# A gated mix of a two-dimensional FFT filter and a GeGLU layer on one Trainium2 core: when a split product is copied, and where one group of an inverse stage is done

## The chip, the core and the metric

One core of a Trainium2 chip. The metric is device time in microseconds (us): the median of three runs of the whole kernel. The profile is of one further execution; its span goes from the first to the last instruction. The engines are TensorE (PE in the profile, its weight loads PEld), VectorE (DVE), ScalarE (ACT), GpSimd (POOL) and SyncE (SP, which here only issues DMAs). Each has its own queue and runs its instructions in order.

## What is computed

From the reference, cut to what matters; x is 2048 tokens of 576 features, `w_gate` and `w_up` are 576 x 4608, `w_down` is 4608 x 576:

```python
def reference(A_x, A_w_r, A_w_i, B_x, B_w_gate, B_w_up, B_w_down, gate_w):
    x = A_x
    g = _sigmoid((x * gate_w).sum(-1, keepdims=True))
    a = _A_ref(x, A_w_r, A_w_i)       # irfft2(rfft2(x) * (w_r + 1j * w_i))
    b = _B_ref(x, B_w_gate, B_w_up, B_w_down)   # (gelu(x wg) * (x wu)) wd
    return g * a + (1 - g) * b
```

All of it is float32. Each float32 factor of a matmul is split into a high part (float32r) and a low part, so one product takes three matmuls: high by high, low by high, high by low.

## The kernel before, in words

**Two strands.** The GeGLU layer fills TensorE; the filter (the spectral work) is done almost wholly by DVE and ACT beside it, as a Python generator from which pieces are taken while the program is written. The order on every engine's queue is therefore fixed by hand at build time (`manual_schedule`).

**The GeGLU strand.** The tokens are two halves of 1024 (p = 0, 1), the 4608 hidden features 18 groups (`PAIRS`) of 256. That makes 36 groups, q = 0 to 35; `PLAN` says how each is done: "c" is a direct group (`conv`, L1411), "s" a group by a Strassen scheme with seven products (`products`, L1197). The plan is 2 c, 10 s, 7 c, 17 s; so there are two Strassen stretches, starting at q = 2 and q = 19 (`starts`), and two direct stretches ahead of them.

A direct group does four hidden blocks (`hidden`, L923): for each of two token blocks tb of 512 and two blocks e of 128 features a gate chain and an up chain (`chain`, L878, 14 matmuls of 512 columns). GELU of the gate chain is done by ACT into `gl`; then `mult` on DVE multiplies it by the up chain's bank and frees that bank, `copy` on ACT makes the high part `hb[:, 0]`, and `low` on DVE (L944) the low part `hb[:, 1]`. A Strassen group does fourteen `seven`s (L1181, seven matmuls each; seven products, two halves s each); at n = 0 ACT copies each half's bank into the bank in which n = 1 goes on adding. A finished pair of hidden blocks goes on the list `pend`; `pop` takes from it and `down` (L973) does the down product: 12 matmuls of 288 columns, an ACT eviction into `stg` (L984) and an accumulating DMA into `yd` (POOL).

**Gaps.** `gap` (L774) is called after the first and third quarter of every chain, after every `seven` and after every `down`. It counts up, then issues (1) what `at(n, ...)` has put down for this count, in order of count and then of entry, (2) one entry of `aux`, (3) pieces of the spectral generator, as long as `credit` is positive. TensorE's work adds to the credit, each piece has a cost (0.69 us, 0.61 us and so on), and the credit is cut to 1.2 (2.0 during the columns) at each gap. A piece that yields None ends the gap. So a "gap later" means behind everything that was put on that engine's queue in between. `seq(key, (n, step), ...)` puts down steps for later gaps, and `due(key)` issues at once those that are still open. A down product calls `due` for both of its hidden blocks; `products` also does so for the last direct pair before its first seven (L1233).

**The spectral strand** (`spectral`, L675): rows forward for each half of the tokens, then `columns` (L255 on; forward column transform, weights, inverse column transform, beside the direct groups q = 12 to 18), then the inverse rows in the last stretch. The tile `til` holds 16 column tiles, four groups d of four. `beside` inside `columns` does the first inverse stage (`four` with sign +1: `_butterfly`, ten DVE instructions) for the groups d = 0 to 2 and stores each with `keep(d)`, four DMAs from til to `bw` in DRAM (L621). For d = 3 the end of `columns` does it: it loads the sources of the second half's Strassen operands into the tile `rows` (`load_part`, 8 DMAs), puts down the loads of the third part for two gaps later (4 DMAs, into tmp and orow), does `four(3, ...)`, `keep(3)`, and notes the count in `kept`:

```python
            for i in range(2):
                load_part(1, i)
            at(2, lambda: load_part(1, 2))
            yield from four(3, range(4), r[:, 0:SW], 1)
            keep(3)
            kept[0] = count[0]
```

Then `operands(1)` (L1051) makes the sums and their high parts (ACT, `sx`, which overwrites the place of `til`) and low parts (DVE). Its `steps` does the sums of part 0, waits until `count` is `kept[0] + HOLD` (HOLD = 5), puts the three high parts of part 2 on a list `acts`, and goes on with the sums of part 1; each piece that it yields first issues one entry of `acts`. After `until(3)`, that is in the last Strassen stretch, `fetch(e)` loads the four tiles of row block e from `bw` (L625), `late_tiles(e)` does the second inverse stage, and `inverse_rows` the rest and the output through `last_rows` (L570, and an accumulating DMA at L571). Before the last group (q = 35) whatever is left of the generator is issued with no GeGLU work between. In the last direct groups `reload_x` (L1404) brings x of the second half through `aux`: `prep_x` (L820) copies the high part on ACT (xhi<-wq and others), and puts down the low part on DVE (L826) for the next gap.

Of the kernel before, what the change touches and what calls it, by code (L numbers as in the profile page):

```python
# [26 lines left out]
SW = 2 * (KF + 1)  # L27
# [136 lines left out]
def _build(nc, tc, a):  # L164
    with ExitStack() as ctx:
# [3 lines left out]
        vec, act, pl, pe = nc.vector, nc.scalar, nc.gpsimd, nc.tensor  # L169
# [10 lines left out]
        _, loc = _block_of_token()  # L180
# [37 lines left out]
        def copy(o, i):  # L218
            act.activation(o, i, AF.Copy)  # L219
# [11 lines left out]
        def rows_tile():  # L231
            return pool.tile([P, ROWS], F32, name="rows", tag="rows")
# [6 lines left out]
        def columns():  # L239
# [141 lines left out]
            n = count[0]  # L381
# [7 lines left out]
            for i in range(2):  # L389
                load_part(1, i)  # L390
            at(2, lambda: load_part(1, 2))
            yield from four(3, range(4), r[:, 0:SW], 1)
            keep(3)
            kept[0] = count[0]

        re, im = slice(0, NK), slice(NK, SW)

# [3 lines left out]
        def four(d, at, sp, sgn):  # L401
            T = tiles()
            yield from _butterfly(vec, lambda i: T[:, d, i], lambda i: T[:, d, i, re], lambda i: T[:, d, i, im],
                                  at, sp, sgn, (0.69, 0.39))
# [204 lines left out]
        def until(n):  # L609
            while phase[0] < n:  # L610
                yield None
# [11 lines left out]
        def fetch(e):  # L623
            for d in range(4):
                nc.sync.dma_start(fetched[d], bw[:, SW * (4 * e + d):SW * (4 * e + d + 1)])  # L625

        def late_tiles(e):

            if e % 2 == 0:
                box[0] = rows_tile()  # L630
            rows = box[0]
            R = row_view(rows)
            x = [tmp[:, SW * i:SW * (i + 1)] for i in range(4)]
            src = list(fetched)
            *tmps, sp = (rows[:, i:i + SW] for i in (UNIT, UNIT + SW, 3 * UNIT, 3 * UNIT + SW))
            o = LEFT.index(e)
            if o:
                for k in range(1, 4):
                    c = 1.0 if o * k == 4 else math.sin(math.pi * o * k / 8)
                    act.activation(tmps[k - 1], src[k], AF.Copy, scale=c)  # L640
                    yield None
                for k in range(1, 4):
                    c, t, y = math.cos(math.pi * o * k / 8), tmps[k - 1], src[k]
                    if o * k == 4:
                        act.activation(x[k][:, re], t[:, im], AF.Copy, scale=-1.0)
                        copy(x[k][:, im], t[:, re])
                    else:
                        vec.scalar_tensor_tensor(x[k][:, re], y[:, re], c, t[:, im], op0=ALU.mult, op1=ALU.subtract)
                        yield 0.39
                        vec.scalar_tensor_tensor(x[k][:, im], y[:, im], c, t[:, re], op0=ALU.mult, op1=ALU.add)  # L650
                        yield 0.39
                    src[k] = x[k]
            n = 0
            for v in _butterfly(vec, lambda i: x[i], lambda i: x[i][:, re], lambda i: x[i][:, im],
                                range(4), sp, 1, (0.69, 0.39), src):
                yield v
                n += 1
                if n == 4 and e < 3:
                    yield None
                    fetch(e + 1)  # L660
            yield None
            s2 = sgn[:, None, :].to_broadcast([P, 2, KF])
            for n in range(2):
                g = 2 * (e % 2) + n
                pl.memset(rows.rearrange("p (c g k) -> p c g k", c=2, g=4)[:, :, g, 2 * KF:], 0.0)
                y = tmp[:, 2 * SW * n:2 * SW * (n + 1)].rearrange("p (t c k) -> p c t k", t=2, c=2)[:, :, :, 0:KF]
                copy(R[:, g, 0, :, 0:KF], y[:, 0])
                vec.tensor_tensor(R[:, g, 1, :, 0:KF], y[:, 1], s2, ALU.mult)
                yield 0.69
            yield None  # L670
# [4 lines left out]
        def spectral(rows):  # L675
# [63 lines left out]
            cols[0] = False  # L739
            yield from operands(1)  # L740
            yield from until(3)
            fetch(0)
            for _ in range(4):
                yield None
# [104 lines left out]
        def seq(key, *steps):  # L849

            q = todo[key] = [fn for _, fn in steps]
            for n, _ in steps:
                at(n, lambda: q and q.pop(0)())

        def due(key):
            q = todo.pop(key, [])
            while q:
                q.pop(0)()
# [64 lines left out]
        def hidden(q, e, tb, mid):  # L923

            i = hn[0]
            hn[0] += 1
            g = gl[i % 2]
            if i == 0:
                pg, pu = first_chains()
                act.activation(g, pg, AF.Gelu_apprx_tanh)  # L930
            else:
                pg = chain(q, e, 0, tb)
                act.activation(g, pg, AF.Gelu_apprx_tanh)
                mid()
                pu = chain(q, e, 1, tb)
            u = take()
            h = hb[u]

            def mult():
                vec.tensor_tensor(g, g, pu, ALU.mult)  # L940
                copy(h[:, 0], g)

            def low():
                vec.tensor_tensor(h[:, 1], g, f(h[:, 0]), ALU.subtract)  # L944

            credit[0] -= 1.22
            seq(("h", i), (1, mult), (3, low))
            return (q, e), u, ("h", i)

        def down_mm(ps, prev, t, part):  # L950
# [188 lines left out]
        def prep_b(q, m, lead=0):  # L1139

            if q >= len(PLAN) or PLAN[q] != "s":
                return
            w = slots[q, m]
            r11, r21, ts, r12, r22 = spots(q)
            x = (r11, r21, ts, r11, r12, r22, r21)[m]

            def high():
                copy(w[:, 256:1024], x)

            def low():  # L1150
                o = w.rearrange("p (c k) -> p c k", c=5)[:, 0:5:2]
                vec.tensor_tensor(o, x.rearrange("p (c k) -> p c k", c=3),  # L1152
                                  f(w[:, 256:1024]).rearrange("p (c k) -> p c k", c=3), ALU.subtract)

            def tail():
                copy(w[0:64, 512:768], x[0:64, 256:512])

            credit[0] -= 0.88
            seq(("b", q, m), (lead + 1, high), (lead + 3, low), (lead + 4, tail))
# [37 lines left out]
        def products(q):  # L1197
# [30 lines left out]
            def add(o, x, v):  # L1228
                vec.tensor_tensor(o, x, v, ALU.add)
                credit[0] -= 0.61  # L1230

            downs = (0, 0, 1, 0, 1, 1, 1) if q in starts else (1, 1, 1, 1, 1, 1, 2)
            if q in starts:  # L1233
                for _, _, key in pend[-1][0][3]:
                    due(key)
            for n, (name, nd) in enumerate(zip(("a11", "a12", "s2", "s1", "s3", "s4", "a22"), downs)):
                if q in starts and n == 0:
                    prep_b(q, 2, -1)
                m = n + 3
                if n in (1, 2):  # L1240
                    total(q, 4 - n)
# [277 lines left out]
```

## Time and profile before

| | us |
|---|---|
| runs | 1337.53, 1338.86, 1337.45 (median 1337.53) |
| the profiled execution, whole | 1338.92 |
| its span, first to last instruction | 1337.1 |
| TensorE (PE) busy | 1325.9 |
| DVE busy | 1141.0 |
| ACT busy | 862.5 |
| POOL busy | 267.3 |

Mean granted TensorE clock 0.998. Busy means that an instruction of the engine is under way; matmuls overlap, so a matmul of 512 columns is shown with some 390 ns though the next starts 227 ns later. Lines L219, L98, L103 and L106 belong to the helpers `copy` and `_butterfly`; there the tile names say which work it is. A row of the timeline gives start, duration, engine, line, operation, tiles out<-in, shape, count, and in brackets how long the engine was idle before and what ended that.

### The profile page before, as it was taken

How to read it: one execution, taken by the hardware profiler on the slowest of the kernel's cores; microseconds unless marked ns; L12 is line 12 of the kernel's file. 1: busy time of each engine (PE TensorE's matmuls, PEld its weight loads, DVE VectorE, ACT ScalarE, POOL GpSimd, SP SyncE). 2: the span in 40 equal slices, each digit the busy share in tenths (PEclk: the TensorE clock that was granted, in tenths of full speed). 3: DMA queues.
4: the chain of work that ended last, by engine and by line, in shares of the span. 5: the costliest groups of instructions: out<-in, count | busy, mean ns of one | idle time of the engine just before them, and what ended most of it. 6: DMA issues, size and time to landing. Idle time of an engine off the chain costs nothing.

```text
span 1337.1 us, 19999 instructions
## 1 busy us (share of the span) xinstructions
PE 1325.9 (99%) x7311; PEld 1172.6 (88%) x7311; DVE 1141.0 (85%) x1621; ACT 862.5 (65%) x1504; POOL 267.3 (20%) x341
## 2 busy tenths in 40 slices
PE   9999999999999999999999999999999999999998
PEld 7888888888888888989888888888888888888888
DVE  6899999899899688899778889999958999996554
ACT  5666766666665546777675776676577667667762
POOL 0011212212122222222211022121132212113211
PEclk9999999999999999999999999999999999999999
DMA  8667777876667978999985576766798676677977
GB/s 310 225 141 153 146 144 131 217 153 127 110 119 163 227 171 192 222 262 240 254 237 164 153 199 129 136 129 129 133 179 194 133 136 130 134 136 141 178 166 177
DMA packets 106146, 227.98 MB, mean 170 GB/s; under 512 B 12224, under 2 KB 19904, under 8 KB 105664
## 3 DMA queue, kind: packets, MB, share of 16 engines
q0 software_dynamic: 45888, 94.52, 45.8%
q1 hardware_dynamic: 60160, 132.18, 30.5%
q8 instruction: 57, 0.93, 0.3%
q14 instruction: 41, 0.34, 0.1%
HBM read 124.88 MB, written 99.39 MB: 168 GB/s over the span
## 4 chain that ended last, share of the span: by engine, by line
PE 90%; DVE 4%; DMA 3%; ACT 2%; issue 1%; SPq 0%; DVEq 0%; ACTq 0%
PE pdn L958 32%; PE pgu L1190 7%; PE pgu L1192 6%; PE pgu L1191 6%; PE pone L1190 6%; PE pone L1192 6%; PE pone L1191 6%; PE pgu L1193 3%; PE pone L1193 3%; PE pgu L883 2%; PE pgu L885 2%; PE pgu L884 2%; PE pone L883 1%; PE pone L885 1%; PE pone L884 1%
## 5 line engine op out<-in xcount | busy, mean ns | idle before, releaser
L971 POOL DMA_DIRECT2D yd<-stg x264 | 225.7, 856 | 897.8 <-ACT stg L984 698.1
L984 ACT ACTIVATE stg<-pdn,omg 128x576 f32<-128x576 f32 x276 | 204.5, 741 | 293.9 <-PE pdn L958 291.8
L958 PE MATMUL pdn<-dn,hb 128*128 128x288 f32 x2352 | 345.9, 295 | 0.8 <-ACT stg L984 0.5
L958 PEld LDWEIGHTS pdn<-dn,hb 128*128 128x128 f32 x2352 | 332.0, 188 | 14.0 <-ACT stg L984 1.3
L219 ACT ACTIVATE gu<-wq 128x768 fp32r<-128x768 f32 (+2 forms) x401 | 253.7, 647 | 52.5 <-DVE gu L1152 31.1
L1152 DVE TENSOR_TENSOR gu<-wq,gu 128x768 fp32r<-128x768 f32 x189 | 180.1, 953 | 49.1 <-ACT gu L219 48.2
L958 PE MATMUL pdn<-dn,hx 128*128 128x288 f32 x1080 | 167.1, 295 | 0.4 <-DVE hx L1215 0.4
L958 PEld LDWEIGHTS pdn<-dn,hx 128*128 128x128 f32 x1080 | 154.7, 188 | 5.3 <-DVE hx L1215 0.6
L1169 DVE TENSOR_TENSOR wq<-wq 128x768 f32<-128x768 f32 x108 | 102.4, 952 | 11.7 <-ACT gu L219 11.6
L883 PE MATMUL pgu<-xhi,gu 128*128 128x512 f32 x212 | 83.2, 392 | 0.9 <-DVE gl L940 0.9
L885 PE MATMUL pgu<-xlo,gu 128*128 128x512 f32 x212 | 82.9, 391 | 0.0
L884 PE MATMUL pgu<-xhi,gu 128*128 128x512 f32 x212 | 82.8, 390 | 0.0
L1190 PE MATMUL pgu<-xhi,gu 128*128 128x512 f32 x160 | 63.4, 396 | 2.7 <-ACT pgu L219 2.7
L1190 PE MATMUL pone<-xhi,gu 128*128 128x512 f32 x164 | 64.3, 392 | 0.0
L1190 PE MATMUL pone<-sx,gu 128*128 128x512 f32 x164 | 64.3, 392 | 0.0
L1192 PE MATMUL pone<-xlo,gu 128*128 128x512 f32 x164 | 64.0, 390 | 0.0
L1192 PE MATMUL pone<-sx,gu 128*128 128x512 f32 x164 | 64.0, 390 | 0.0
L1191 PE MATMUL pone<-xhi,gu 128*128 128x512 f32 x164 | 63.9, 390 | 0.0
L1191 PE MATMUL pone<-sx,gu 128*128 128x512 f32 x164 | 63.9, 390 | 0.0
L1193 PE MATMUL pone<-sx,gu 128*128 128x512 f32 x164 | 63.8, 389 | 0.0
L1192 PE MATMUL pgu<-xlo,gu 128*128 128x512 f32 x160 | 63.1, 394 | 0.0
L1191 PE MATMUL pgu<-xhi,gu 128*128 128x512 f32 x160 | 63.0, 394 | 0.0
(262 smaller groups left out, 2794.4 us busy)
## 6 DMA issues: line engine op xcount, KB each, us to landing
yd<-stg POOLq DMA_DIRECT2D x276, 288.0 KB, 4.8
wq<-ws SPq DMA_DIRECT2D x108, 384.0 KB, 4.5
wq<-wd SPq DMA_DIRECT2D x72, 288.0 KB, 5.2
wq<-wgu SPq DMA_DIRECT2D x16, 640.0 KB, 5.8
colm<-col POOLq DMA_DIRECT2D x32, 256.0 KB, 7.4
misc<-wf SPq DMA_DIRECT2D x16, 290.0 KB, 5.9
hx<-til SPq DMA_DIRECT2D x64, 72.5 KB, 5.3
tmp<-wf SPq DMA_DIRECT2D x16, 290.0 KB, 6.3
```

The costliest lines, as they stand in the source:

```text
L219: act.activation(o, i, AF.Copy)
L883: pe.matmul(ps, w[:, 0, k, c], xhi[tb][:, k], start=k == 0, stop=False)
L884: pe.matmul(ps, w[:, 1, k, c], xhi[tb][:, k], start=False, stop=False)
L885: pe.matmul(ps, w[:, 0, k, c], xlo[tb][:, k], start=False, stop=False)
L958: pe.matmul(ps[half], h[:, l, c], d[:, k, half * HD:(half + 1) * HD], start=part == 0 and n == 0, stop=part == 1 and n == 2)
L971: pl.dma_start(yd[u], o, accum_op=ALU.add)
L984: put(u, lambda o: act.activation(o.rearrange("p (c k) -> p c k", c=2), v[:, :, 0:HD], AF.Copy, scale=omg[:, u:u + 1]), i == 0)
L1152: vec.tensor_tensor(o, x.rearrange("p (c k) -> p c k", c=3), f(w[:, 256:1024]).rearrange("p (c k) -> p c k", c=3), ALU.subtract)
L1190: pe.matmul(ps, hi, xh[:, t], start=start and t == 0, stop=False, skip_group_check=True)
L1191: pe.matmul(ps, lo, xh[:, t], start=False, stop=False, skip_group_check=True)
L1192: pe.matmul(ps, hi, xl[:, t], start=False, stop=False, skip_group_check=True)
L1193: pe.matmul(ps, tl, xt, start=False, stop=stop, skip_group_check=True)
```

## The change

Three edits. In `hidden`, the high part is copied one gap behind the product, no longer in the same gap, and the low part comes in the fourth gap instead of the third. In `products`, at the start of a stretch the last direct pair's open steps are issued ahead of n = 1 instead of ahead of n = 0. And `columns` no longer does the first inverse stage for d = 3: it stores the group as it is, and a new `last_group` in the last stretch loads these four tiles into the tile `rows`, does the stage there and stores them, ahead of `fetch(0)`.

```diff
             at(2, lambda: load_part(1, 2))
-            yield from four(3, range(4), r[:, 0:SW], 1)
             keep(3)
             kept[0] = count[0]
+            yield None
...
+        def last_group():
+
+            r = rows_tile()
+            x = [r[:, SW * i:SW * (i + 1)] for i in range(5)]
+            cs = [slice(SW * (4 * e + 3), SW * (4 * e + 4)) for e in range(4)]
+            for i in range(4):
+                nc.sync.dma_start(x[i], bw[:, cs[i]])
+            for _ in range(4):
+                yield None
+            yield from _butterfly(vec, lambda i: x[i], lambda i: x[i][:, re], lambda i: x[i][:, im],
+                                  range(4), x[4], 1, (0.69, 0.39))
+            yield None
+            for i in range(4):
+                nc.sync.dma_start(bw[:, cs[i]], x[i])
+            yield None
...
             yield from until(3)
+            yield from last_group()
             fetch(0)
...
             def mult():
                 vec.tensor_tensor(g, g, pu, ALU.mult)
-                copy(h[:, 0], g)
...
-            seq(("h", i), (1, mult), (3, low))
+            seq(("h", i), (1, mult), (2, lambda: copy(h[:, 0], g)), (4, low))
...
+            held_back = pend[-1][0][3] if q in starts else ()
             downs = (0, 0, 1, 0, 1, 1, 1) if q in starts else (1, 1, 1, 1, 1, 1, 2)
-            if q in starts:
-                for _, _, key in pend[-1][0][3]:
-                    due(key)
             for n, (name, nd) in enumerate(zip(("a11", "a12", "s2", "s1", "s3", "s4", "a22"), downs)):
                 if q in starts and n == 0:
                     prep_b(q, 2, -1)
+                if q in starts and n == 1:
+                    for _, _, key in held_back:
+                        due(key)
```

## Rows read from the trace of the kernel before

**Rows 1.** The page, busy time by engine: us, share of the span, instructions.
```profile
PE 1325.9 (99%) x7311; PEld 1172.6 (88%) x7311; DVE 1141.0 (85%) x1621; ACT 862.5 (65%) x1504; POOL 267.3 (20%) x341
```
**Rows 2.** Who waited for whom, whole span: us in total, times, longest.
```profile
PE pgu L1190 <- ACT pgu L219: 2.7, 2, 2.0
...
ACT hb L219 <- DVE gl L940: 33.5, 18, 3.9
```
**Rows 3.** The chain of waits, 724 to 740 us: start, us, what.
```profile
726.50 0.96 DVE wq L1169
...
728.12 0.61 DVE gl L940
...
728.75 0.63 ACT hb L219
729.38 1.47 ACT gu L219 x2
730.85 0.49 ACT pgu L219
```
**Rows 4.** Timeline of PE at the second stretch start.
```profile
728.72 0.39 PE L1192 MATMUL pone<-xlo,gu 128*128 128x512 f32 x1
728.95 0.39 PE L1193 MATMUL pone<-sx,gu 128*128 128x512 f32 x1
731.38 0.50 PE L1190 MATMUL pgu<-xhi,gu 128*128 128x512 f32 x1 [2.04 <-ACT pgu L219]
...
735.36 0.40 PE L1190 MATMUL pgu<-xhi,gu 128*128 128x512 f32 x1
```
**Rows 5.** Busy time in one us of it; PEclk is the granted clock.
```profile
733.00:734.00 1.00, 1.00 (x4) 0.81 (x3) 1.00 (x3) 0.21 (x1) 0.00 (x0) 0.50 0.00 0
```
**Rows 6.** Timeline of PE at the first stretch start.
```profile
79.44 0.39 PE L1193 MATMUL pone<-sx,gu 128*128 128x512 f32 x1
80.47 0.50 PE L1190 MATMUL pgu<-xhi,gu 128*128 128x512 f32 x1 [0.64 <-ACT pgu L219]
```
**Rows 7.** Timelines of DVE and PE, one closing direct pair of q = 1.
```profile
43.05 0.69 DVE L944 TENSOR_TENSOR hb<-gl,hb 128x512 fp32r<-128x512 f32 x1
...
44.63 3.35 PE L958 MATMUL pdn<-dn,hb 128*128 128x288 f32 x24
```
**Rows 8.** DVE groups by line, 694.5 to 704.2 us: busy us, mean ns.
```profile
L98 DVE TENSOR_TENSOR til<-til 128x580 f32<-128x580 f32 x3 | 2.3, 759 | 0.1
L103 DVE TENSOR_TENSOR til<-til 128x290 f32<-128x290 f32 x4 | 1.6, 454 | 0.0
L106 DVE TENSOR_TENSOR til<-rows,til 128x580 f32<-128x580 f32 x2 | 1.5, 758 | 0.0
```
**Rows 9.** Timeline of ACT at the end of the columns.
```profile
704.54 0.62 ACT L219 ACTIVATE xhi<-wq 128x512 fp32r<-128x512 f32 x1
...
713.25 1.16 ACT L219 ACTIVATE sx<-tmp 128x512 fp32r<-128x512 f32 x2 [4.56 <-DMA wq<-ws]
```
**Rows 10.** SP's timeline of the loads; two of the stores by themselves, issue and landing.
```profile
691.81 4.35 SPq L1049 DMA_DIRECT2D rows<-xs  x8
...
L621 SPq DMA_DIRECT2D bw<-til x1: 327/327/327, 702.7 to 702.7; - x1
...
DMA to landing us min/median/max: 6.7/6.7/6.7
...
L621 SPq DMA_DIRECT2D bw<-til x1: 451/451/451, 704.4 to 704.4; - x1
...
DMA to landing us min/median/max: 8.6/8.6/8.6
```
**Rows 11.** Timeline of PE, second token block of q = 18: its tenth matmul.
```profile
708.94 0.39 PE L883 MATMUL pone<-xhi,gu 128*128 128x512 f32 x1
```
**Rows 12.** The output rows of the spectral work (ACT); first matmul of the last group.
```profile
L570 ACT ACTIVATE tmp<-rows,gs x8: 847/866/882, 1216.7 to 1255.0; 128x640 f32<-128x640 f32 x8
...
1284.45 0.40 PE L1190 MATMUL pone<-xhi,gu 128*128 128x512 f32 x1
```

## The prediction

> **What bounds the kernel now.** I read the engine table first: TensorE is busy for 99% of the span [rows 1]. So time is won only where TensorE stands still or runs at its lower clock, and the list of waits says where that is [rows 2]: its largest entry is 2.7 us, in two waits, of the first matmul into a pgu bank at L1190 for an ACT copy into that bank. Both stand at the start of a Strassen stretch. ACT, by contrast, waits 33.5 us for the direct pairs' product L940 [rows 2], and that alone costs nothing, because ACT is not the bound.
>
> The chain of waits around the second stretch start shows why it stalls [rows 3]: the DVE product of the last direct pair ends at 728.73, ACT's copy hb stands at the head of its queue until then, two weight copies (gu) follow, and only then, at 730.85, the copy into pgu which TensorE needs. TensorE's rows give the price [rows 4]. Matmuls of 512 columns start 0.23 us apart, so the next one was due at 729.18 and came at 731.38: 2.20 us. After that the granted clock is 0.50, that is 1.2 instead of 2.4 GHz [rows 5], and ten matmuls take 3.98 us (731.38 to 735.36) instead of 2.27: 1.71 us. At the first stretch start the next matmul was due at 79.67 and came at 80.47 [rows 6]: 0.80 us, with no loss of clock. All together 0.80 + 2.20 + 1.71 = 4.7 us.
>
> **The change, part by part.** *The held-back pair.* At a stretch start the last pair's product, copy and low part are no longer forced ahead of the first two sevens; the product comes in the first gap, the copy in the second. The pgu copy of half 0 is issued between them, so the 0.63 us copy that waits for DVE no longer stands before it. The two gu copies (1.47 us) still do [rows 3]. They read sums of L1169, the second of which ends at 727.46 [rows 3]; from there 1.47 us of gu and 0.5 us of pgu copy end at 729.4, 0.2 us behind 729.18. So this part wins between 3.9 (0.2 left over, no clock lost) and nothing; I take 4.5 of the 4.7, because the product and its 0.63 us copy are what stands in that chain besides. The low part is needed only in the down product behind n = 2, four sevens after it is issued: nothing.
>
> *Copy and low part one gap later in every direct pair.* There are 36 of these; the 18 that close a token block matter, because their low part is used one pair later. The tightest that I found is at 43.05 [rows 7]: the low part ends at 43.73; its first use is the eleventh of 24 matmuls that start at 44.63, 0.14 us apart, at 46.0. That is 2.3 us of cover. A gap is half a chain, 6 x 0.23 = 1.4 us. So nothing here; were the cover gone, at most 0.7 us (one DVE instruction) for one or two of the 18. Nor does it win anything: what TensorE needs of a direct pair at once is the product, which frees the bank, and its place is unchanged.
>
> *The inverse stage leaves the columns.* It takes ten DVE instructions out of 695 to 704: four of 0.76 us at L98 (the row has the three that write til), four of 0.45 at L103, two of 0.76 at L106 [rows 8], 6.4 us in all. DVE is not the bound there; by itself this gives nothing. But two things move with it. First, `kept` is set in the gap in which the columns end instead of four gaps later. Numbering the gaps of the last direct group (q = 18) from its first chain, the columns end in gap 5 (the product L940 of its first pair is issued in that gap, and L98 stands right behind it in DVE's rows). The stage lasts to gap 9, HOLD is 5, so now ACT's copies into sx begin in gap 14; with the change in gap 10. With a credit of 1.2 and sums of 0.61, two of them are issued in that gap. In gap 11 ACT is given the copy of x for the second token block (xhi<-wq); now it runs at 704.54, ahead of the sx copies, which start at 713.25 after 4.56 us of waiting [rows 9]. **With the change it stands behind two of them.** Second, the four stores of `keep(3)` go on SP's queue ahead of the four loads of the last source part, where they now go behind.
>
> What do the sx copies wait for? They overwrite til, so for the last of the four stores: issued at 704.4, landed 8.6 us later at 713.1 [rows 10], 0.2 us before ACT moves. The row names the DMA wq<-ws, the release that the profile infers. They also need their own load, the first copy the 13th, the second the 14th of these 16 transfers. TensorE needs xhi<-wq at its tenth matmul of the second token block, 708.94 [rows 11]. When does the 14th land? The same 16 transfers are in hand from 691.81 on; the second store, 14th in the order before, was issued at 702.73 and landed 6.7 us later, at 709.4 [rows 10]. As the four stores (290 KB each, against 256 KB for a load) now stand all among the first fourteen, I take 710.0. Then the second sx copy ends at 710.55 (two take 1.16 us [rows 9]), xhi<-wq at 711.15, and TensorE stands still from 708.94 to 711.15: **2.2 us**. That is what it stood still at the stretch start, after which the clock fell; so 1.7 us more: 3.9. Bounds: nothing, if the 14th lands by 707.8 (copy done before 708.94); 5.3 + 1.7 = 7.0 us, if it lands with the last of the sixteen, at 713.1 (copies done at 714.25). I take 3.9, since the row of the 14th transfer is the nearest.
>
> Behind the copy its low part L826 runs on DVE (0.69 us, a subtraction of the size of the one in [rows 7]) and is needed two matmuls later: at the lower clock that is 0.85 us, nothing.
>
> *The same stage in the last stretch.* It adds four loads, six gaps of pause, the ten DVE instructions and four stores before `fetch(0)`. A gap there is a seven or a down, about 1.6 us (14 sevens of 7 x 0.23 us and 8 downs of 12 x 0.14). Six pauses and 5.7 us of credit, at under one us of credit per gap, make 10 to 14 gaps, 16 to 22 us. The spectral work now ends with the last L570 at 1255.01, and the last group, before which it has to be done, starts at 1284.45 [rows 12]: 29 us free. So nothing; were it late, each gap too many would hold TensorE some 1.6 us. On SP the load of `fetch(0)` that reads a stored block waits for that store, and group loads queue behind it: between nothing and the 2.04 us that the late pgu copy cost at the stretch start [rows 4], the longest wait that TensorE has for another engine. I take nothing, since ACT's wait of 4.56 us [rows 9] cost TensorE no idle time either.
>
> **The sum.** -4.5 + 3.9 = -0.6 us. The profiled execution took 1338.9 us (its span 1337.1 and 1.8 around it), 1.4 above the median of the runs shown; the difference carried to the median gives 1336.9 us.
>
> **The rivals.** *No new stall.* If the 14th transfer lands by 707.8, the gain stays: 1337.5 - 4.5 = 1333.0 us. For it: with the stores issued early, SP's queue is never without work, and the loads of the last part could pass stores. Against it: the stores in the rows landed in the order of their issue, 709.4 before 713.1 [rows 10]. The Trainium skill ("DMA: Bandwidth & Descriptors", section "Two DMAs through the same engine are not ordered") says that of two transfers on a queue the later may finish its write before the earlier; by that rule a load could land before the stores and the sum would be this rival's, -4.5; in the two stores' rows no such passing shows. The first sx copy waits for the last store all the same. A short stall that leaves the clock alone (under 1 us, as at 79.67 to 80.47 [rows 6]) belongs here too: up to 1334.0.
>
> *The new stall is larger than the old.* The second sx copy waits on the last of the sixteen transfers or longer. From the point where the 14th lands after 713.4, the stall is over 5.6 us, and with 1.7 for the clock over 7.3: more than 4.5 + 2.7. Landing at 714, as a transfer or so more ahead of it would make it: 6.2 + 1.7 - 4.5 = +3.4, 1340.9 us. For it: two stores took from 709.4 to 713.1 [rows 10], 1.8 us each, and all four now go first. Against it: all sixteen were in by 713.1 in the old order.
>
> *The change does not reach its stall.* If the two gu copies wait as long as before, the pgu copy is late anyway, by up to the same 2.2 us and the clock: with the new stall (3.9, less the 0.8 of the first start) 1337.5 + 3.1 = 1340.6. Against it: their sums end 3.4 us before the pgu copy began.
>
> **How the numbers follow.** A difference within 0.2% (2.7 us) is about what a measurement of this kernel can't tell from no change. The forecast, a new stall of 1 to 5 us with its clock in place of the old ones (between -2.6 and +2.5 us), has 0.59; no or a short new stall 0.30; the larger stall 0.08 and the unreached one 0.03, together 0.11. The range reaches from the second case's 1332.8 (4.7 won in full) to 1340.0, the forecast's upper bound (7.0 - 4.5 = +2.5 us): beyond it lie the slower cases and what other work may win. Of its own, the forecast would range from 1334.9 to 1340.0.
>
> **What would show it.** Right: no wait of TensorE for the pgu copy at either stretch start and a granted clock of 1.00 behind the second; a new wait of PE L883 for ACT xhi some 17 us ahead of the second stretch, of about 2 us, with a clock of 0.50 after it; in ACT's rows sx<-tmp before xhi<-wq; the stores L621 issued at 696 instead of 702; the last L570 some 15 us later, and no wait behind it. Wrong: no such wait of L883 (then about 1333), or waits of PE pdn L958 for DVE hb L944 in the direct groups, or a wait in the last stretch before 800 us or behind 1284.

## The result and the profile after

The changed kernel takes 1341.55 us (median of 8 runs, 1340.92 to 1344.53), the kernel before, run beside it, 1338.76 (8 runs, 1337.45 to 1339.10). The ratio is 1.0028, 95% interval 1.0019 to 1.0037: slower by 0.28%. Forecast were 1336.9 and a range that ends at 1340.0. The profiled execution of after took 1343.29 us, its span 1341.5, against 1338.92 and 1337.1: it lies 1.7 us above the median of its runs, so its rows may show more than the median run lost.

In the changed file the lines stand 16 or 17 further down (the kernels of the experiments differ from this by one or two more): L883 is L900, L885 L902, L940 L957, L944 L960, L958 L974, L984 L1000, L1049 L1065, L1169 L1185, L1190 L1206.

The table of waits, whole span (us in total, times, longest), to be held against [rows 2]:

```profile
PE pone L900 <- ACT xhi L219: 3.2, 1, 3.2
...
PE pgu L900 <- DVE gl L957: 1.3, 2, 1.0
PE pdn L974 <- ACT stg L1000: 1.2, 2, 1.0
PE pdn L974 <- DVE hb L960: 0.7, 1, 0.7
PE pgu L1206 <- ACT pgu L219: 0.6, 2, 0.4
```

The wait for pgu has shrunk from 2.7 to 0.6 us, and a wait for xhi of 3.2 us is new. The three rows between them are the direct groups beside the columns (566 to 700 us); in the profile before that stretch has two such rows only:

```profile
PE pgu L883 <- DVE gl L940: 0.9, 2, 0.6
PE pdn L958 <- ACT stg L984: 0.5, 1, 0.5
```

So it waits 3.2 us there instead of 1.4.

**The new stall**, on TensorE, where [rows 11] ran through:

```profile
709.76 0.39 PE L902 MATMUL pone<-xlo,gu 128*128 128x512 f32 x1
713.33 0.80 PE L900 MATMUL pone<-xhi,gu 128*128 128x512 f32 x1 [3.18 <-ACT xhi L219]
...
718.62 0.57 PE L901 MATMUL pone<-xhi,gu 128*128 128x512 f32 x1
719.03 0.39 PE L902 MATMUL pone<-xlo,gu 128*128 128x512 f32 x1
```

The matmul was due 0.23 us behind 709.76, at 709.99, and came at 713.33: 3.34 us. From there to 719.03 thirteen matmuls take 5.70 us instead of 2.95: 2.75 us of lower clock, and the busy table by single microseconds shows its end (the granted clock is the third number from the end; it is 1.00 at 711 to 712 and 0.59 in the next):

```profile
718.00:719.00 1.00, 1.00 (x3) 0.76 (x3) 0.97 (x2) 0.00 (x0) 0.00 (x0) 0.50 0.55 143
719.00:720.00 1.00, 1.00 (x6) 0.80 (x5) 1.00 (x3) 0.00 (x0) 0.00 (x0) 1.00 0.72 226
```

Together 6.1 us. What stands ahead of xhi<-wq on ACT is the pair of sx copies, as the prediction had it, each waiting, by the release that the profile infers, for its own load:

```profile
710.04 0.63 ACT L219 ACTIVATE sx<-tmp 128x512 fp32r<-128x512 f32 x1 [4.36 <-DMA tmp<-xs]
712.13 0.63 ACT L219 ACTIVATE sx<-tmp 128x512 fp32r<-128x512 f32 x1 [1.45 <-DMA tmp<-xs]
712.66 0.61 ACT L219 ACTIVATE xhi<-wq 128x512 fp32r<-128x512 f32 x1
```

On SP's queue the stores now go ahead of the last four loads; the landing of the last store (it and the third: 8.4 and 8.5 us behind the issue) and of the first two tmp loads (7.8 and 8.7 us):

```profile
698.65 3.52 SPq L621 DMA_DIRECT2D bw<-til  x4
702.21 3.56 SPq L1065 DMA_DIRECT2D tmp<-xs  x3
```
```profile
L621 SPq DMA_DIRECT2D bw<-til x2: 800/1034/1267, 700.0 to 700.9; - x2
...
DMA to landing us min/median/max: 8.4/8.4/8.5
```
```profile
L1065 SPq DMA_DIRECT2D tmp<-xs x2: 1122/1194/1267, 702.2 to 703.4; - x2
...
DMA to landing us min/median/max: 7.8/8.2/8.7
```

The last store was in at 700.9 + 8.4 = 709.3, the 13th transfer (the first tmp load) at 702.2 + 7.8 = 710.0 and the 14th at 703.4 + 8.7 = 712.1: the last two are the starts of the two sx copies.

**The stretch starts.** At the first one TensorE runs through, where [rows 6] had 0.64 us of idle time:

```profile
80.02 0.39 PE L1209 MATMUL pone<-sx,gu 128*128 128x512 f32 x1
80.25 0.39 PE L1206 MATMUL pgu<-xhi,gu 128*128 128x512 f32 x1
```

At the second two short waits are left of [rows 4], with the clock at 1.00:

```profile
736.13 0.39 PE L1209 MATMUL pone<-sx,gu 128*128 128x512 f32 x1
736.91 0.50 PE L1206 MATMUL pgu<-xhi,gu 128*128 128x512 f32 x1 [0.39 <-ACT pgu L219]
737.25 0.40 PE L1207 MATMUL pgu<-xhi,gu 128*128 128x512 f32 x1
...
738.42 0.40 PE L1209 MATMUL pgu<-sx,gu 128*128 128x512 f32 x1
738.98 0.50 PE L1206 MATMUL pgu<-xhi,gu 128*128 128x512 f32 x1 [0.16 <-ACT pgu L219]
```

The first is 736.91 - 736.36 = 0.55 us behind its due time, the second 738.98 - 738.65 = 0.33, and the matmul after each comes 0.34 instead of 0.23 us later: 1.1 us in all. The chain of waits is that of [rows 3], without the copy hb ahead of gu:

```profile
733.74 0.97 DVE wq L1185
...
734.79 1.58 ACT gu L219 x2
736.37 0.48 ACT pgu L219
```

**The balance** of the two profiled executions: the starts gave 4.7 - 1.1 = 3.6 us, the new stall takes 6.1, the waits beside the columns 3.2 - 1.4 = 1.8. That is +4.3 us of the 4.4 by which the times differ.

**The last stretch** has no wait of TensorE for another engine between 740 and 1320 us. The spectral work ends later (compare [rows 12]; of the second row the last four matmuls' first start is that of the last group):

```profile
L570 ACT ACTIVATE tmp<-rows,gs x16: 848/872/887, 994.6 to 1280.1; 128x640 f32<-128x640 f32 x16
...
L1206 PE MATMUL pone<-xhi,gu x4: 389/391/397, 1288.9 to 1291.2; 128*128 128x512 f32 x4
```

It had 29 us to spare and has 8.8 left.

### The profile page after: what moved, and what is told of

Same layout as the page of the kernel before. It is cut to its first block, busy times and chain, and to the rows that moved or that the text cites. A ratio compares the mean times of both kernels' runs of the same rounds, so it can differ in the third digit from the quotient of the medians.

```text
span 1341.5 us, 20025 instructions
## 1 busy us (share of the span) xinstructions
PE 1327.6 (99%) x7311; PEld 1173.4 (87%) x7311; DVE 1141.3 (85%) x1621; ACT 863.4 (64%) x1504; POOL 268.0 (20%) x341
## 4 chain that ended last, share of the span: by engine, by line
PE 92%; DMA 3%; ACT 2%; DVE 2%; issue 1%; SPq 0%; DVEq 0%; ACTq 0%
PE pdn L974 32%; PE pgu L1206 6%; PE pone L1206 6%; PE pgu L1208 6%; PE pgu L1207 6%; PE pone L1208 6%; PE pone L1207 6%; PE pgu L1209 3%; PE pone L1209 3%; PE pgu L900 3%; PE pgu L902 3%; PE pgu L901 3%; PE pone L900 1%; PE pone L901 1%; PE pone L902 1%; PE pone L286 1%
## 5 line engine op out<-in xcount | busy, mean ns | idle before, releaser
L1000 ACT ACTIVATE stg<-pdn,omg 128x576 f32<-128x576 f32 x276 | 204.6, 741 | 297.9 <-PE pdn L974 296.9
L974 PE MATMUL pdn<-dn,hb 128*128 128x288 f32 x2352 | 346.3, 295 | 2.2 <-ACT stg L1000 1.2
L974 PEld LDWEIGHTS pdn<-dn,hb 128*128 128x128 f32 x2352 | 332.0, 188 | 15.9 <-ACT stg L1000 1.9
L974 PE MATMUL pdn<-dn,hx 128*128 128x288 f32 x1080 | 167.1, 295 | 0.4 <-DVE hx L1231 0.4
L974 PEld LDWEIGHTS pdn<-dn,hx 128*128 128x128 f32 x1080 | 154.6, 188 | 5.3 <-DVE hx L1231 0.6
L1185 DVE TENSOR_TENSOR wq<-wq 128x768 f32<-128x768 f32 x108 | 102.4, 952 | 6.0 <-ACT gu L219 6.0
L900 PE MATMUL pgu<-xhi,gu 128*128 128x512 f32 x212 | 83.1, 392 | 1.3 <-DVE gl L957 1.3
L902 PE MATMUL pgu<-xlo,gu 128*128 128x512 f32 x212 | 82.9, 391 | 0.0
L901 PE MATMUL pgu<-xhi,gu 128*128 128x512 f32 x212 | 82.8, 391 | 0.0
L1206 PE MATMUL pone<-xhi,gu 128*128 128x512 f32 x164 | 64.3, 392 | 0.0
L1206 PE MATMUL pone<-sx,gu 128*128 128x512 f32 x164 | 64.3, 392 | 0.0
L1206 PE MATMUL pgu<-xhi,gu 128*128 128x512 f32 x160 | 62.9, 393 | 0.6 <-ACT pgu L219 0.6
L1206 PE MATMUL pgu<-sx,gu 128*128 128x512 f32 x160 | 62.7, 392 | 0.0
```

The source lines that it names most:

```text
L900: pe.matmul(ps, w[:, 0, k, c], xhi[tb][:, k], start=k == 0, stop=False)
L901: pe.matmul(ps, w[:, 1, k, c], xhi[tb][:, k], start=False, stop=False)
L902: pe.matmul(ps, w[:, 0, k, c], xlo[tb][:, k], start=False, stop=False)
L974: pe.matmul(ps[half], h[:, l, c], d[:, k, half * HD:(half + 1) * HD], start=part == 0 and n == 0, stop=part == 1 and n == 2)
L1000: put(u, lambda o: act.activation(o.rearrange("p (c k) -> p c k", c=2), v[:, :, 0:HD], AF.Copy, scale=omg[:, u:u + 1]), i == 0)
L1206: pe.matmul(ps, hi, xh[:, t], start=start and t == 0, stop=False, skip_group_check=True)
```

## The experiments

Before has, in the three series of experiments (1 to 4, 5 to 8, 9 to 11), medians of 1338.85, 1337.77 and 1338.63 us (26, 28 and 27 runs); each ratio below is against the runs made on the same chip in the same series.

**1. The two GeGLU edits alone.** From after, the stage goes back into the columns:

```diff
+            yield from four(3, range(4), r[:, 0:SW], 1)
             keep(3)
             kept[0] = count[0]
-            yield None
...
-            yield from last_group()
```

> The change without its third edit: the inverse stage of the last group stays in the columns; the copy a gap later and the held-back pair are kept. Theory A (the stage's move is what costs, because the copy xhi<-wq now stands behind sx copies that wait for the stores): no wait of L883 for ACT xhi near 709 us; the 6.1 us lost there are gone, the stretch starts keep their gain of 3.6 us, the columns their 1.6 us of loss: about 2 us under the kernel before, near 1336.8. Theory B (the copy one gap later in all direct pairs is what costs): still 2 to 4 us over the kernel before, with waits of TensorE for hb or stg in the direct groups.

Measured: 1336.97 us (11 runs, 1336.52 to 1338.45), ratio 0.9991 (0.9983 to 1.0000). The wait for xhi near 709 us is gone. The profiled execution is the slowest of the eleven, 1338.45, and has a wait of 1.47 us that the profile after lacks; experiment 8 comes back to it.

**2. The stage's move alone.** From before, only the edits to `columns` and `last_group`.

```diff
-            yield from four(3, range(4), r[:, 0:SW], 1)
             keep(3)
             kept[0] = count[0]
+            yield None
...
+            yield from last_group()
```

> The kernel before with the third edit alone: the inverse stage of the last group in the last stretch, copies and held-back pair as before. Theory A: a wait of L883 for ACT xhi of about 3 us near 709 us with the clock at 0.50 behind it, 5 to 6 us; the stall at the second stretch start stays or shrinks: 2 to 6 us over the kernel before. Theory B: no slower than the kernel before.

Measured: 1343.92 us (5 runs), ratio 1.0036 (1.0023 to 1.0050). In its table of waits the new and the old stall stand together:

```profile
PE pone L900 <- ACT xhi L219: 4.7, 1, 4.7
PE pgu L1207 <- ACT pgu L219: 2.7, 2, 2.0
```

So the loss belongs to this edit, and does not need the others: +4.8 us by the ratio, and -1.2 from experiment 1, make +3.6, about what the whole change did (+3.8 by its ratio).

**3. The change, with part 2's high sums held longer.** If ACT's order is the cause, holding them for nine gaps after `kept` puts xhi<-wq ahead again and undoes the stall, with the stores as early as in after.

```diff
-                while count[0] < kept[0] + HOLD:
+                while count[0] < kept[0] + (HOLD if p == 0 else 9):
```

> The change with one number altered: the second half's operands wait 9 gaps behind kept instead of 5, so the sx copies are issued in gap 14 as in the kernel before, behind xhi<-wq. Theory A: no wait of L883 for ACT xhi; about 6 us less than the change, 2 us under the kernel before. Theory B: as slow as the change.

Measured: 1337.62 us (11 runs), ratio 0.9993 (0.9984 to 1.0002). ACT's rows have the copy first, and TensorE has no wait for it:

```profile
705.73 0.62 ACT L219 ACTIVATE xhi<-wq 128x512 fp32r<-128x512 f32 x1
...
709.55 1.15 ACT L219 ACTIVATE sx<-tmp 128x512 fp32r<-128x512 f32 x2
```

This one number takes back 3.9 us by the medians (4.7 by the ratios), not the 6 that were expected from the profiled execution of after. The stall is the order on ACT's queue, not the early stores by themselves and not the work moved into the last stretch, both of which are still there.

**4. The held-back pair alone**, from before:

```diff
-            if q in starts:
-                for _, _, key in pend[-1][0][3]:
-                    due(key)
...
+                if q in starts and n == 1:
+                    for _, _, key in held_back:
+                        due(key)
```

> The kernel before with the second edit alone: the last direct pair's steps are no longer forced before the first seven, but copy and product are still in one gap. Theory A: ACT's copy hb still waits for DVE's product ahead of the pgu copy, so the second stretch start keeps most of its 3.8 us: 0 to 2 us under the kernel before. If the forcing alone was the cause, both starts are cured and the time is 3 to 4.7 us under it.

Measured: 1335.87 us (10 runs, 1335.54 to 1336.67), ratio 0.9980 (0.9971 to 0.9989). It beats both kernels. The first start has no wait; the second still waits, because product and copy share a gap, and the copy hb waits for DVE between the two gu copies:

```profile
726.85 0.85 ACT L219 ACTIVATE gu<-wq 128x768 fp32r<-128x768 f32 x1 [0.82 <-PE pone L1208]
728.05 0.63 ACT L219 ACTIVATE hb<-gl 128x512 fp32r<-128x512 f32 x1 [0.35 <-DVE gl L956]
728.59 0.83 ACT L219 ACTIVATE gu<-wq 128x768 fp32r<-128x768 f32 x1
729.32 0.58 ACT L219 ACTIVATE pgu<-pone 128x512 f32<-128x512 f32 x1
```
```profile
729.95 0.50 PE L1206 MATMUL pgu<-xhi,gu 128*128 128x512 f32 x1 [1.31 <-ACT pgu L219]
```

**5. The change, with the copy of x two gaps earlier**, so that it goes ahead of the sx copies without moving these.

```diff
+            z = (0, 2, 4, 6, 8) if tb else (0, 2, 4, 6, 10)
-                i = (0, 2, 4, 6, 10).index(n) if n in (0, 2, 4, 6, 10) else None
+                i = z.index(n) if n in z else None
```

> The change, with the fifth x copy of the second token block (xhi<-wq) issued in gap 9 instead of 11, so that it stands ahead of the sx copies; the sx copies stay in gap 10 and wait as long. Theory A (TensorE stood still only because of that one copy's place in ACT's queue): no wait of L900 for ACT xhi, ACT still waits some 4 to 6 us at sx<-tmp, and the time is that of the variant with HOLD 9, 1337 to 1338. Rival (ACT's long wait costs wherever x stands, through hb, stg or gl behind it): a wait of similar size comes up within 8 us, and 1340 or more.

Measured: 1342.38 us (6 runs, 1339.50 to 1344.68), ratio 1.0030 (1.0018 to 1.0042): no better than the change. In the profiled execution the wait for xhi is gone and others stand in its place, most of them in the down product behind that chain (1.40 us of the row, at 718.16, is there; the rest is the direct group of experiment 8):

```profile
PE pdn L974 <- DVE hb L960: 2.1, 2, 1.4
```

From 708.48 to 713.99 us ACT does three sx copies and otherwise waits for their loads; what follows in its queue (dn, hb, then the low parts on DVE) is late whichever instruction it is. So it is not enough to move xhi out of the way: the waiting copies delay whatever stands behind them. That execution is the fastest of the six, 1339.50; what the slower ones lose besides has no trace.

**6. The stage moved, held for nine gaps, the first edit undone.** Experiment 4 and the stage's move:

```diff
-                while count[0] < kept[0] + HOLD:
+                while count[0] < kept[0] + (HOLD if p == 0 else 9):
...
+            yield from last_group()
```

> Second and third edit with HOLD 9 for the second half, the first edit undone: the stage is moved, the sx copies come behind xhi<-wq, copies and products stay in one gap. If moving the stage is worth something of its own (6.4 us of DVE work less ahead of the second stretch), it lies under the variant with the held-back pair alone (1335.9); if not, within 0.7 us of it. If the stage's eight transfers in the last stretch cost something, over it.

Measured: 1336.29 us (11 runs), ratio 0.9986 (0.9977 to 0.9995), against 0.9980 for experiment 4: the 6.4 us of DVE work taken out of the columns win nothing, and they cost nothing in the last stretch, as far as these runs can tell (the two intervals overlap).

**7 and 8. The first edit in its two halves**, each added to experiment 4: the copy one gap later (7), the low part one gap later (8).

```diff
-            seq(("h", i), (1, mult), (3, low))
+            seq(("h", i), (1, mult), (2, lambda: copy(h[:, 0], g)), (3, low))   # 7; copy taken out of mult
+            seq(("h", i), (1, mult), (4, low))                                  # 8; copy left in mult
```

> The held-back variant (1335.9) with only the copy of all direct pairs a gap later and the low part in its old gap. If the late copy is what costs in the columns (it stands behind evictions and pushes the column copies back), losses of L899 and L973 at 576, 636 and 669 us grow by about 1.6 us, no wait for hb at 581: 1337 to 1337.5. If the late low part is it, 1335.5 to 1336.

> The held-back variant (1335.9) with only the low part of all direct pairs a gap later and the copy in its old gap. If the late copy is what costs: a wait of pdn for hb near 581 us of at most 1 us and otherwise the losses of the kernel before, 1336 to 1336.5. If the late low part is it: 1337 to 1337.5, with waits of pdn for DVE hb.

Measured: 7: 1335.78 us (11 runs), ratio 0.9982 (0.9973 to 0.9991); 8: 1337.29 us (11 runs, 1336.91 to 1338.96), ratio 0.9998 (0.9989 to 1.0007). The late copy is worth nothing as a sum: its profile waits 2.3 instead of 1.4 us beside the columns (for stg and gl) and 0.5 instead of 1.3 at the second start. The late low part costs 1.4 us against experiment 4, and 1.5 against 7 in the same series. One place where it costs is seen in the profile after, in one of the direct groups beside the columns. DVE:

```profile
574.96 0.68 DVE L957 TENSOR_TENSOR gl<-gl,pgu 128x512 f32<-128x512 f32 x1
...
580.45 0.68 DVE L960 TENSOR_TENSOR hb<-gl,hb 128x512 fp32r<-128x512 f32 x1
```

and TensorE's down product, which reads that low part:

```profile
581.19 0.53 PE L974 MATMUL pdn<-dn,hb 128*128 128x288 f32 x2 [0.70 <-DVE hb L960]
```

Before, the same low part stood ahead of seven instructions (one of the weights, dn, and six of the columns) that are now between the product gl and it, and the down product ran in one piece:

```profile
575.90 0.68 DVE L940 TENSOR_TENSOR gl<-gl,pgu 128x512 f32<-128x512 f32 x1
577.28 0.69 DVE L944 TENSOR_TENSOR hb<-gl,hb 128x512 fp32r<-128x512 f32 x1 [0.70 <-ACT hb L219]
```
```profile
579.98 1.75 PE L958 MATMUL pdn<-dn,hb 128*128 128x288 f32 x12
```

The whole group runs 0.94 us earlier in the profile after, so the two places are counted from the product: 577.28 - 575.90 = 1.4 us behind it before, 580.45 - 574.96 = 5.5 now. One gap later is 4.1 us here.

A second place is shown by the trace of experiment 1 (the slowest of its runs), in the first direct groups. There DVE has an instruction that waits for a load, and the low part, which in the profile before stands ahead of it (at 22.34 us, the load being waited for until 26.19), now stands behind it:

```profile
26.17 0.83 DVE L819 SCALAR_TENSOR_TENSOR tmp<-rows,misc 128x640 f32<-128x640 f32 x1 [4.96 <-DMA rows<-xn]
...
27.79 0.69 DVE L959 TENSOR_TENSOR hb<-gl,hb 128x512 fp32r<-128x512 f32 x1
```
```profile
28.53 2.12 PE L973 MATMUL pdn<-dn,hb 128*128 128x288 f32 x14 [1.47 <-DVE hb L959]
```

In the traces of after and of experiment 8 the load was in earlier (DVE goes on at 24.99 and 24.72 us), and there is no such wait. This is the fault of the third edit once more, on another engine: work put behind an instruction that waits for a DMA. That it makes up the rest of the 1.4 us, and the spread of some 2 us in the runs of experiments 1, 3 and 8, is likely and not shown, with one trace of it.

**9. Experiment 7 with the second weight copy behind the pgu copy** at a stretch start:

```diff
-                prep_b(q + m // 7, m % 7, (0, 1, 0, 0, 0, 0, 2)[n])
+                prep_b(q + m // 7, m % 7, ((1 if q in starts else 0), 1, 0, 0, 0, 0, 2)[n])
```

> The held-back pair with the copy a gap later and the low part in its old gap, and besides, at a stretch start, the second weight copy gu put one gap later, so that ACT makes the pgu copy of the first half ahead of it. If the 1 us still lost at the second start is the one gu copy ahead of the pgu copy: no wait of PE L1206 for ACT pgu at the second start, about 1 us under the run with the copy late, 1334.8 us. If it is the sums of DVE, or if the gu copy is then missed by the seven that reads it: another wait at the start, no gain, 1335.8 or more.

Measured: 1335.69 us (11 runs), ratio 0.9982 (0.9973 to 0.9990): no gain. The first half's bank comes in time, and the second half waits instead, since the gu copy and two sx copies now stand ahead of its copy:

```profile
PE pgu L1205 <- ACT pgu L219: 0.8, 1, 0.8
```

ACT runs there without a break from 726.88 to 733 us, so what is left at the second start is probably ACT's load, not the place of one copy; no run takes work off ACT there.

**10. All three edits, repaired**: HOLD 9 for the second half, the low part in its old gap.

```diff
-            seq(("h", i), (1, mult), (2, lambda: copy(h[:, 0], g)), (4, low))
+            seq(("h", i), (1, mult), (2, lambda: copy(h[:, 0], g)), (3, low))
...
-                while count[0] < kept[0] + HOLD:
+                while count[0] < kept[0] + (HOLD if p == 0 else 9):
```

> All three edits, but the low part in its old third gap and the second half's high sums held for nine gaps instead of five. If the stall behind the sx copies and the late low part are the whole of what the change cost: no wait for xhi, the direct groups as before, and the time of the held-back pair's edit alone, 1335.5 to 1336.3 us, some 2.5 us under before. If moving the inverse stage costs or wins something of its own, it shows here: over 1337, or under 1335.

Measured: 1336.24 us (11 runs), ratio 0.9985 (0.9976 to 0.9994). With its two faults mended the change is 2 us faster than before, and no faster than the held-back pair alone.

**11. The first edit alone**, with the last pair forced ahead of n = 0 as before:

```diff
-                copy(h[:, 0], g)
...
-            seq(("h", i), (1, mult), (3, low))
+            seq(("h", i), (1, mult), (2, lambda: copy(h[:, 0], g)), (4, low))
```

> The first edit alone, with the last pair forced at the stretch starts as before and the inverse stage where it was. If the late low part costs some 1.4 us wherever the rest stands: about 1.4 us over before, with a wait of PE pdn for DVE hb in the direct groups of the columns, and the starts lose their 4.7 us as before. If the cost needs the other edits (work of the columns shifted by them): same as before, within 0.5 us. If the copy one gap later gives ACT and DVE room: under before.

Measured: 1339.21 us (11 runs), ratio 1.0012 (1.0003 to 1.0021): some 1.6 us over before, near the 1.4 expected. Its direct groups wait 3.2 us in the same three rows as after. Its second start has the wait of [rows 4] to the hundredth, and not the lower clock of [rows 5]:

```profile
733.21 0.50 PE L1205 MATMUL pgu<-xhi,gu 128*128 128x512 f32 x1 [2.04 <-ACT pgu L219]
```
```profile
734.00:735.00 1.00, 1.00 (x6) 0.81 (x5) 1.00 (x3) 1.00 (x3) 0.00 (x0) 1.00 0.00 0
```

**12. The kernel before, unchanged**, since that raised the question whether its clock falls in every run. Its 81 runs in the three series of experiments stand in two groups with nothing between 1338.2 and 1338.6 us: 38 with a median of 1337.45 and 43 with 1339.03. All 30 runs with a mean granted clock of 0.998 are in the upper one, and 22 of the 23 with 1.000 in the lower.

> The kernel before, unchanged, profiled once more. The runs of before stand in two groups, around 1337.4 and around 1339.0 us. If what parts them is whether the granted clock falls behind the 2.04 us wait at the second stretch start: a profiled execution near 1337.4 has the wait, a clock of 1.00 behind it and matmuls 0.23 us apart; one near 1339.0 has 0.50 there and ten matmuls in some 4 us, as in the first profile. If the groups are something else (loads, the end): the clock behind the wait doesn't go with the time.

Measured: one profiled execution of 1338.78 us, clock 0.998, with 0.50 behind the wait, as in the first profile:

```profile
733.00:734.00 1.00, 1.00 (x4) 0.81 (x3) 1.00 (x3) 0.14 (x1) 0.00 (x0) 0.50 0.00 0
```

No execution of the lower group was profiled, so that the groups are parted by this fall is not shown outright. What speaks for it: both profiles of the upper group have the fall; the groups lie 1.58 us apart, and it costs 1.71; where that wait is 1.31 us or less and the low part is in its old gap (experiments 4, 6, 7, 9, 10), 53 of 54 runs lie between 1335.38 and 1336.93; and the two kernels with the wait but without the fall in their trace fit the lower group: 1337.45 and the 1.8 us more beside the columns make 1339.25, where the profiled execution of experiment 11 took 1339.17; 1337.45 and the stall of experiment 2 (4.87 us late and 1.54 of clock) make 1343.86, where it took 1344.12.

## Why the prediction was wrong

**Which steps failed, by the runs.** The median, 1341.55, lies 4.65 us above the 1336.9 that were forecast. The largest part is the first term, -4.5 for the held-back pair: carried to 1337.53 it promises 1333.0 for that edit by itself, and experiment 4 measured 1335.87, 2.9 short. The second is the low part, put at nothing: 1.4 (experiment 8). The new stall, put at 3.9, is worth 3.9 us in the medians of after and experiment 3, and 4.7 by their ratios: 0 to 0.8. That is 4.3 to 5.1 in all.

**The mechanism of the new stall was right, and its size in the profiled execution was not.** The stall came at the matmul that was named, behind the two copies that were named, and experiments 2 and 3 show that this order is its cause. For the term "2.2 us idle and 1.7 of clock, 3.9" this execution has 3.34 and 2.75, 6.1, within the bounds of 0 to 7.0. Half of the error is the landing of the 14th transfer. Forecast was 710.0 with TensorE's matmul due at 708.94; the matmul is now due at 709.99, so that the forecast would be 711.0, and it landed at 712.1. (The stores went out at 698.65, not at 696 as said.) The sign of the reason was right: all sixteen transfers landed in the order of issue. But one row of the old order gives no spread: by issue and landing in the traces of the six kernels with these stores ahead, that load was in at 712.1 (after), 712.9 (experiment 2), 710.0 (3), 710.1 (5), 710.3 (6) and 708.2 (10). So 710.0 was a fair middle, and that the stall's worth in the medians comes out at 3.9 is in part luck. The rest of the error is the clock: 1.71 us was carried over as if it came with every such stall.

**"Copy and low part one gap later: nothing" failed.** The late low part cost about 1.4 us (experiment 8). The step was the cover: 2.3 us of it, found at 43.05 [rows 7] and called the tightest, was held against "a gap is half a chain, 1.4 us". That is TensorE's measure of a gap. For a DVE instruction a gap is what is put on DVE's queue between the two places: beside the columns that was seven instructions and 4.1 us, and at 26 us it was an instruction waiting for a load. The bound of "at most 0.7 us" rested on the same step. Of the 1.8 us by which the waits beside the columns grew in the profile after, the low part has the 0.7 for hb; the rest, for stg and gl, comes with the late copy, as in experiment 7. The half about the copy was right as a sum, by experiment 7 against 4.

**The held-back pair** won 3.6 of 4.7 us in the profile after, where 4.5 were forecast. The 0.2 us left over for the first half is 0.55, because in the chain the two gu copies took 1.58 and not 1.47 us and began 0.08 behind their sum; the second half's copy, with hb and two more gu copies ahead of it, was not in the sum at all (0.33), nor was the slower first step after a wait (0.11 each).

**The base** is where most of the missing 2.9 us lies. The 1.71 us of clock is a loss of the profiled execution, 1338.92. The median of the three runs, 1337.53, belongs to the lower group; to subtract it there, "the difference carried to the median", counts a gain that these runs, if experiment 12 is read rightly, did not have to give. From the profiled execution the same sum gives 1338.3; the 5.0 us by which its counterpart, 1343.29, lies above are the stall (6.1 - 3.9 = 2.2), the groups beside the columns (1.8) and the starts (0.9).

**What held**: the 6.4 us of DVE work win nothing by leaving the columns (experiment 6), and the stage costs nothing in the last stretch, by TensorE's empty table of waits there. The spectral work ends 25 us later, not 15, which would matter if the cover were not 29.

**The rivals.** No new stall is refuted for the change as it stands, and in the profile after nothing shows the passing of one transfer by another on which it partly stood: the last store landed at 709.3 and the two loads behind it at 710.0 and 712.1. By the Trainium skill ("DMA: Bandwidth & Descriptors", section "Two DMAs through the same engine are not ordered") a later transfer may finish first; this trace shows no such case. The larger stall gave 1340.9, near the 1341.55 measured, but that is luck: it asked for a landing after 713.4, which did not come in this trace (712.1, or 711.1 in the times of before), and the 6.1 us measured exceed the 4.7 of the old stalls only for the clock's part. The unreached stall is refuted by the profile after, where the matmul behind the pgu copy is 0.55 us late and not 2.2, and by the time of experiment 4.

## What to carry to other kernels

A copy that may wait for a DMA blocks everything behind it on an in-order engine, so a counter that sets when it is issued (here `kept`) is part of any edit that moves work ahead of it: list what changes places in the queue, and place the copy behind the load's slowest landing, not its usual one. The cover of a step moved by one slot is measured on the queue of its own engine, in the busiest stretch in which it occurs and wherever that queue waits for a load, and not by TensorE's time in a quiet one. And a loss seen in one profiled execution is subtracted from that execution's time: if the runs stand in two groups, find out first to which of them the loss belongs, and if the profiled execution is slower than the median, price a term by runs with and without it.

## What the runs showed of the hardware

The fall of the clock does not go with the length of the wait alone. The same 2.04 us wait at the second start was followed by 0.50 in both profiles of before and by 1.00 in experiments 2 and 11. After 3.18 us of idle time the lower clock took thirteen matmuls (2.75 us lost); after 4.71 us in experiment 2 it took seven, from 714.12 to 717.25 us, 3.13 instead of 1.59: 1.5 us lost.

```profile
714.12 0.79 PE L900 MATMUL pone<-xhi,gu 128*128 128x512 f32 x1 [4.71 <-ACT xhi L219]
...
717.25 0.40 PE L902 MATMUL pone<-xlo,gu 128*128 128x512 f32 x1
```

In none of the three waits of 0.8 to 1.4 us looked at (1.31 in experiment 4, 0.8 in experiment 9, 1.40 in experiment 5) was a fall seen. The Trainium skill ("TensorE: Matmul & The Clock Gate", "Part 1: The HAM clock gate") says that the monitor behind the clock runs on its own and does not start anew with a kernel, so that the point of a change varies; a wait that has a fall in one execution and none in another agrees with that.
